# Q inside attention: four direct products, or seven products of sums

## The chip, the cores and the metric

The kernel runs on one core of a Trainium2 chip. The core has a matrix engine (TensorE: PE for its matmuls, PEld for its weight loads), VectorE (DVE), ScalarE (ACT), GpSimd (POOL) and a queue engine (SyncE, SP) that here issues nearly all DMAs. Matmuls read SBUF and write PSUM, of which the kernel uses eight banks of 128 x 512 floats. The metric is the time of one execution on the device in microseconds (us), lower is better. The kernel before takes 3028.04 us (median of 3 runs, 3027.93 to 3028.24).

## The reference

One transformer block over 2048 tokens of width 576, in float32. Six rows (shift, scale and gate, twice) come from `silu(c) @ w_mod`. Then

- `h = layernorm(x) * (1 + ca) + sa`
- `q = h @ wq`: 32 heads of 128; keys and values are the last 512 rows of a cache, 16 heads of each, so two query heads share a key and value head
- `p = softmax(q k^T / sqrt(128))`, `o = p v`, `x = x + ga * (o @ wo)`
- `h = layernorm(x) * (1 + cb) + sb`, and `x = x + gb * ((sigmoid(h @ w_gate) * (h @ w_up)) @ w_down)` with 4608 inner columns

## The kernel before

**Precision.** Float32 operands are split into a high part, rounded by ACT to the matmul's type, and the low rest (DVE or POOL subtracts). A product of two operands is three matmuls: high x low, low x high, high x high.

**Stages.** A short start, attention, output projection, and the gated MLP. Output projection and MLP already work with seven products where a 2 x 2 block product would take eight; the sums of their weights are made in the background, during attention. They are not changed.

**Attention.** Tokens come in four blocks of 512, in two halves of two blocks. The unit of order is a *block* `b`: one head over one block of tokens, 128 in all (`NBLK`), in the order of the list `seq`. A block has four *tiles* of 128 tokens, and the stage's loop runs over 512 tiles: `for n in range(NLO, N + TPB + 4)`, one *step* each, `N` = 512. `b, i = divmod(n, 4)`. In step `n` the program writes, in this order:

1. whatever is registered for the step with `at_n`
2. a quarter of Q of block `b + 2` (`qproj`): for a block 14 matmuls, four K-chunks of 128 rows at three each, and two for the remaining 64 rows. They accumulate in one bank (`qp`); after the last, ACT copies the high part, scaled by `QSCALE`, and DVE subtracts the low one (tile `qt`, two buffers)
3. the three score matmuls of tile `n + 2` and the row maximum on DVE (`neg<-st`)
4. four transposes of the exponentials of tile `n`, and their split (`ptt<-st`, ACT and then DVE)
5. the exponential of tile `n + 2` on ACT, with row sums; at a block's last tile DVE takes reciprocals (`rs<-sum`)
6. a quarter of PV of block `b - 1` (`pv`): three matmuls of 512 columns, over the tile `ptt` of that whole block, of which there are two. After the fourth quarter DVE multiplies the result by the reciprocals (`ov<-ot,rb`)
7. whatever is registered for the end of the step with `at_late`

Four banks (tag `st`) go round between scores and transposes, two (`ot`) between the PV of successive blocks, and one (`wo`) serves the background's small matmuls.

**The divisors.** The reciprocals lie along partitions, and PV's result needs them along columns. So SP stores them to DRAM (`put_rs`, tensor `rscr`) and loads them back spread over all partitions (`get_rs`, tile `rb`). SP works its queue in order; the load waits there until the store has landed.

**Q's weights.** For each head and each half, `load_q` fetches 576 x 128 weights, ACT makes the high part (`wa<-raw`) eight steps before their first use, and POOL the low part (two instructions) seven steps before.

**Background.** Between these, 79 weight jobs (36 `ab`, 9 `tail`, and 34 *wide* ones: 16 `wo`, 18 `down`) load weights into *rooms*, SBUF space of the four x blocks which is free during attention (tiles `x`), make sums and splits on POOL and ACT (`bg_sums`, `bg_split`), and store them to DRAM (`bg_store`). A loop (`free = {0: 9, ...`) writes out at which step each job starts, by when its room is free and by a due time (`due`) that paces them.

**What sets the order.** The tile framework draws the waits from what each instruction reads and writes, and places instructions on each engine as they become free by its own estimate; `keep_order` and `pin` fix an instruction behind all that the program wrote earlier for that engine. Every POOL instruction of the background is fixed so. The matmuls of Q, scores, transposes and PV are not. Nearly all instructions pass through one helper at line 36, so the profile shows L36 and they are told apart by their tiles.

## Time and profile before

| what | value |
|---|---|
| median of three runs | 3028.04 us |
| the profiled execution: its span, first to last instruction | 3026.5 us |
| the median less that span | 1.5 us |
| granted TensorE clock over the span | 0.999 |
| attention (start of the stage's loop to the output projection's first matmul, by TensorE's timeline) | ends at 1419.8 us |
| PE, DVE, ACT, POOL busy, of the span | 99%, 69%, 56%, 55% |
| Q matmuls in the groups | 1524 + 254, and 12 + 2 in the bank `wo` |

The profile's rows name an instruction by engine, operation, and out<-in by the program's tiles. `qp<-hTm,wa` are Q's matmuls (`hTt` for the 64 rows), `st<-kt,qt` scores, `st<-ident,pp` transposes, `ot<-ptt,vs` PV. A matmul's own duration includes its way through the array, which overlaps the next one's; the distance between starts is what it costs. "SPq" is SP's queue.

### The profile page before, as it was taken

How to read it: one execution, taken by the hardware profiler on the slowest of the kernel's cores; microseconds unless marked ns; L12 is line 12 of the kernel's file. 1: busy time of each engine (PE TensorE's matmuls, PEld its weight loads, DVE VectorE, ACT ScalarE, POOL GpSimd, SP SyncE). 2: the span in 40 equal slices, each digit the busy share in tenths (PEclk: the TensorE clock that was granted, in tenths of full speed). 3: DMA queues.
4: the chain of work that ended last, by engine and by line, in shares of the span. 5: the costliest groups of instructions: out<-in, count | busy, mean ns of one | idle time of the engine just before them, and what ended most of it. 6: DMA issues, size and time to landing. Idle time of an engine off the chain costs nothing.

```text
span 3026.5 us, 49171 instructions
## 1 busy us (share of the span) xinstructions
PE 3006.8 (99%) x16644; PEld 2592.7 (86%) x16644; DVE 2088.4 (69%) x3685; ACT 1695.8 (56%) x3424; POOL 1666.3 (55%) x1558
## 2 busy tenths in 40 slices
PE   8999999999999999999999999999999999999999
PEld 7888888888888888888999988888888888888888
DVE  6666666677666666667888867666666876666667
ACT  5666666657666676555444654444444544444443
POOL 2334457634577887412555127766655566655565
PEclk9999999999999999999999999999999999999999
DMA  4677777776777777775547656555555565555554
GB/s 127 189 197 217 196 224 227 227 210 183 207 233 236 240 248 247 211 215 177 193 159 306 224 189 192 155 155 166 168 148 144 161 204 140 143 148 142 144 138 119
DMA packets 485788, 571.32 MB, mean 189 GB/s; under 512 B 52000, under 2 KB 434208, under 8 KB 476832
## 3 DMA queue, kind: packets, MB, share of 16 engines
q1 hardware_dynamic: 484400, 567.65, 63.1%
q8 instruction: 132, 2.16, 0.3%
q14 instruction: 120, 0.98, 0.1%
q10 hardware_dynamic: 1136, 0.53, 0.1%
HBM read 394.33 MB, written 173.70 MB: 188 GB/s over the span
## 4 chain that ended last, share of the span: by engine, by line
PE 94%; DVE 2%; issue 1%; POOL 1%; DMA 1%; ACT 1%; SPq 0%; POOLq 0%; DVEq 0%; ACTq 0%
PE a L36 21%; PE st L36 18%; PE w L36 13%; PE qp L36 13%; PE ot L36 11%; PE c L36 11%; PE b L36 5%; DVE x L36 1%; POOL x L36 1%; PE wo L36 1%; SPq L36 0%; DVE ptt L36 0%; ACT pp L36 0%; DVE neg L36 0%; DVE hc L36 0%
## 5 line engine op out<-in xcount | busy, mean ns | idle before, releaser
L36 DVE TENSOR_TENSOR x<-w,x 128x288 f32<-128x288 f32 x964 | 421.4, 452 | 249.4 <-PE w L36 246.8
L36 PE MATMUL a<-hc,sw 128*128 128x512 f32 x2016 | 583.4, 395 | 1.4 <-DVE v L36 1.3
L36 DVE TENSOR_REDUCE neg<-st 128x1 f32<-128x512 f32 x512 | 352.4, 688 | 275.6 <-PE st L36 274.9
L36 ACT ACTIVATE ptt<-st 128x512 fp32r<-128x512 f32 x512 | 306.0, 598 | 391.0 <-PE st L36 390.0
L36 PE MATMUL ot<-ptt,vs 128*128 128x512 f32 x1536 | 483.5, 423 | 1.8 <-DVE ptt L36 1.7
L36 PE MATMUL st<-kt,qt 128*128 128x512 f32 x1536 | 443.4, 395 | 0.4 <-ACT pp L36 0.4
L36 PE MATMUL qp<-hTm,wa 128*128 128x512 f32 x1524 | 440.5, 398 | 2.3 <-DVE hTm L36 1.2
L36 DVE TENSOR_TENSOR ptt<-st,ptt 128x512 fp32r<-128x512 f32 x512 | 351.9, 688 | 126.6 <-ACT ptt L36 126.3
L36 PEld LDWEIGHTS a<-hc,sw 128*128 128x128 f32 x2016 | 356.4, 188 | 41.6 <-DVE v L36 2.8
L36 ACT ACTIVATE pp<-st,neg 128x512 f32<-128x512 f32 x512 | 350.4, 684 | 43.7 <-DVE neg L36 42.6
L36 ACT ACTIVATE sw<-sr 128x384 fp32r<-128x384 f32 x504 | 257.9, 519 | 189.1 <-issue 90.0
L36 POOL TENSOR_TENSOR sw<-sr,sw 128x256 fp32r<-128x256 f32 x245 | 200.4, 819 | 282.8 <-ACT sw L36 282.6
L36 PEld LDWEIGHTS st<-kt,qt 128*128 128x128 f32 x1536 | 286.7, 188 | 66.9 <-ACT pp L36 1.1
L36 PEld LDWEIGHTS w<-wh,hl 128*128 128x128 f32 x1776 | 297.2, 188 | 51.2 <-DVE x L36 2.7
L36 PEld LDWEIGHTS qp<-hTm,wa 128*128 128x128 f32 x1524 | 281.5, 188 | 69.5 <-DVE qt L36 7.1
L36 PE MATMUL w<-wh,hl 128*128 128x288 f32 x1776 | 327.5, 296 | 0.4 <-DVE x L36 0.3
L36 POOL TENSOR_TENSOR x<-x 128x256 f32<-128x256 f32 (+3 forms) x342 | 254.4, 763 | 117.8 <-DMA x<-in_B_w_up_dram 58.6
L36 PEld LDWEIGHTS st<-ident,pp 128*128 128x128 f32 x2048 | 254.3, 140 | 70.4 <-ACT pp L36 0.8
L36 PE MATMUL st<-ident,pp 128*128 128x128 f32 x2048 | 307.0, 273 | 0.5 <-DVE ptt L36 0.3
L36 PE MATMUL c<-hc,sw 128*128 128x512 f32 x1008 | 302.9, 394 | 0.0
L36 DVE TENSOR_TENSOR sw<-sr,sw 128x256 fp32r<-128x256 f32 x259 | 189.9, 733 | 141.0 <-ACT sw L36 113.2
L36 PEld LDWEIGHTS ot<-ptt,vs 128*128 128x128 f32 x1536 | 252.9, 190 | 30.7 <-DVE ptt L36 4.2
(239 smaller groups left out, 5043.6 us busy)
## 6 DMA issues: line engine op xcount, KB each, us to landing
sr<-wsc SPq DMA_DIRECT2D x504, 192.0 KB
wh<-dsc SPq DMA_DIRECT2D x144, 288.0 KB
dsc<-x SPq DMA_DIRECT2D x34, 1008.0 KB
vr<-oscr SPq DMA_DIRECT2D x32, 1024.0 KB
rb<-rscr SPq DMA_DIRECT2D x126, 256.0 KB
wsc<-x SPq DMA_DIRECT2D x36, 896.0 KB
oscr<-ov SPq DMA_DIRECT2D x63, 512.0 KB
wosc<-x SPq DMA_DIRECT2D x32, 1008.0 KB
```

The costliest lines, as they stand in the source:

```text
L36: i = got(*args, **kw)
```

## The change

In 30 *units* (all but the first eight blocks) Q is made for two heads and two blocks of tokens together. With the weights of the two heads as rows and the two halves of 512 K-rows as columns, the weights are A11, A12, A21, A22, the normalized tokens B11, B21, B12, B22, and the four results come from seven products of six matmuls instead of four times twelve; the 64 remaining rows add two matmuls to four of the products.

- The sums of the tokens (T1 to T4) are made once for each half, split, and stay in SBUF (the *planes*: the former `hTm` tiles, two further tiles for T1 and T2, and for T3 the fourth x block's space). The sums of the weights (S1 to S4) are made for each unit by POOL, each factor is split, high by ACT, low by POOL or (products 1 and 4) DVE.
- The products accumulate in the banks `qp` ("x") and `wo` ("y"); DVE adds them up over temporaries in SBUF and the last three blocks' Q is split from there. `QSCALE` moves into the keys.
- `QUOTA` says how many of a unit's 50 matmuls each of 14 steps gets; PV takes two steps of six matmuls instead of four of three, in those steps where Q has one or none.
- The exponentials lie in a ring of six tiles instead of two blocks of four, so one PV in three is cut into pieces.
- The divisors' store and load are written one step earlier each, since PV ends two steps earlier.
- Three rooms instead of four; the planner is written anew, jobs start at step 22 instead of 9, sums one step earlier after the load. The x rows for the second half go into rooms 0 and 1.
- The first two weight loads of the output projection go from 34 and 32 steps before the loop's end to 9 and 8, and the fourth x block's load to 9. One matmul is added ahead of the output projection.

The diff, cut to its core:

```diff
     def qproj(b, part):
...
-        lo, hi = n * part // 4, n * (part + 1) // 4
+        lo, hi = [n * i // 4 if b < 2 else (0, 0, 6, 13, 14)[i] for i in (part, part + 1)]
...
+    QSEQ = (("A11", "B11"), ("A12", "B21"), ("S2", "T2"), ("S3", "T3"), ("A22", "T4"), ("S1", "T1"), ("S4", "B22"))
+    QTAIL = {1: (0, 0), 4: (1, 0), 5: (1, 1), 6: (2, 1)}
...
+    def u_sum(u, to):
...
+        op = nc.gpsimd.tensor_add if to == "S1" else nc.gpsimd.tensor_sub
+        pin(op(UA[u, to], UA[u, x0], UA[u, x1]))
...
+    def u_hi(u, j):
+        t = USW[u, j] = wp.tile([P, 4, P], F32R, tag="sw", name="sw", bufs=4)
+        keep_order(nc.scalar.activation(t[:, 0:2], UA[u, QSEQ[j][0]], AF.Copy))
+
+    def u_lo(u, j):
+        t = USW[u, j]
+        eng = nc.vector if j in (1, 4) else nc.gpsimd
+        pin(eng.tensor_sub(t[:, 2:4], UA.pop((u, QSEQ[j][0])) if j > 5 else UA[u, QSEQ[j][0]], f32(t[:, 0:2])))
...
+    def u_out(b, eng):
+        t, c = q_tile(b), u_temp("c")
+        keep_order(nc.scalar.activation(t[:, 0, :], c, AF.Copy))
+        pin(eng.tensor_sub(t[:, 1, :], c, f32(t[:, 0, :])))
+
+    def u_end(u, j, n):
+        b = b_of(u)
+        x, y = UB.get((u, "x")), UB.get((u, "y"))
+        if j == 0:
+            keep_order(nc.scalar.activation(u_temp("m1"), y, AF.Copy))
+        elif j == 1:
+            t = q_tile(b)
+            keep_order(nc.scalar.activation(t[:, 0, :], y, AF.Copy))
+            nc.vector.tensor_sub(t[:, 1, :], y, f32(t[:, 0, :]))
+        elif j in (2, 3):
+            nc.vector.tensor_add(u_temp("u2" if j == 2 else "w"), x if j == 2 else y, u_temp("m1"))
+        else:
+            nc.vector.tensor_add(u_temp("c"), y if j == 4 else x, u_temp({4: "u2", 5: "w", 6: "m1"}[j]))
+            at_late(n + 3 if j == 6 else n, u_out, b + j - 3, nc.vector if j == 4 else nc.gpsimd)
+
+    def u_items(u):
+        for j, (a, c) in enumerate(QSEQ):
+            bank = "x" if j in (2, 5, 6) else "y"
...
+            fresh = j in (0, 2, 3)
...
+    QUOTA = (6, 6, 1, 0, 6, 6, 0, 0, 6, 6, 1, 0, 6, 6)
...
+    def u_some(n):
+        u, k = divmod(n - (TPB * b_of(0) - 10), 4 * TPB)
...
     def expo(n):
...
-                at_late(n - 1, put_rs, b)
-                at_late(n + 1, get_rs, b)
+                at_late(n - 2, put_rs, b)
+                at_late(n, get_rs, b)
...
     def transp(n):
...
+            PTT.append(at.tile([P, 6, 2, KT, P], F32R, tag="ptt", name="ptt", bufs=1))
...
+    def pv(b, part):
...
+        s0 = TPB * b % 6
+        pieces = [(0, s0, TPB)] if s0 + TPB <= 6 else [(0, s0, 6 - s0), (6 - s0, 0, s0 + TPB - 6)]
...
-    for hh in range(3, NH):
-        at_n(max(q_first(hh) - 12, -6), load_q, hh)
-        at_n(q_first(hh) - 8, split_q, hh)
-        at_n(q_first(hh) - 7, split_q_lo, hh)
...
+    for u in range(len(units)):
+        n = TPB * b_of(u) - 10
...
+        for i in range(4):
+            at_n(n - 5 + i, u_sum, u, f"S{i + 1}")
...
+        for j, m in enumerate((-4, -3, -1, 0, 3, 6, 8)):
+            at_n(n + m, u_hi, u, j)
+            at_n(n + m + 1, u_lo, u, j)
...
-    free = {0: 9, 1: 9, 2: 7, 3: 7}
-    n, due = 9, 9.0
...
+    LIFE = {"ab": (9, None), "tail": (13, None), "wo": (11, 6), "down": (11, 6), "mod": (12, None)}
...
+    n, due = 22, 22.0
...
-            at_n(n + 4 + part, bg_sums, k, part)
+            at_n(n + (4 if kind == "tail" else 3) + part, bg_sums, k, part)
...
-        due = max(due, n - 2) + {"ab": 4.6, "tail": 7.6}.get(kind, 5.9)
+        due = max(due, n - 2) + {"ab": 3.3, "tail": 5.4}.get(k[0], 4.3)
...
     for s in range(2):
-        at_n(N - 34 + 2 * s, w_load, 0, s)
+        at_n(N - 9 + s, w_load, 0, s)
...
+        u_some(n)
...
-        if ok(b - 1):
+        if ok(b - 1) and i < 2:
             pv(b - 1, i)
...
+    first = fpsum("b", 1, [P, BLK])
+    nc.tensor.matmul(first, VHL[0, 0][:, 0, 0, :], WHL[0, 0][0].rearrange("p a b -> p (a b)")[:, :BLK],
+                     start=True, stop=True)
```

More of the change, by code (lines that the diff above doesn't have):

```diff
@@ L97, in raw_tile @@
     def raw_tile(shape):
-        return wp.tile(shape, F32, tag="raw", name="raw", bufs=4)
+        return wp.tile(shape, F32, tag="raw", name="raw", bufs=2)
     def f32(ap):
@@ new lines, in adaln_block_kernel @@
+    QUOTA = (6, 6, 1, 0, 6, 6, 0, 0, 6, 6, 1, 0, 6, 6)
+    stream = {}
+    def u_some(n):
+        u, k = divmod(n - (TPB * b_of(0) - 10), 4 * TPB)
+        if not 0 <= u < len(units) or k >= len(QUOTA):
+            return
+        if k == 0:
+            stream[u] = u_items(u)
+        for _ in range(QUOTA[k]):
+            j = next(stream[u])
+            if j is not None:
+                u_end(u, j, n)
+        if k == len(QUOTA) - 1:
+            assert next(stream.pop(u), "end") == "end"
@@ new lines, in adaln_block_kernel @@
+    mod_at, mod_due = {}, [30, 52, 80, 116]
+    n, due = 22, 22.0
+    while jobs or wide or mods:
+        assert n < N - 30, (n, len(jobs), len(wide), len(mods))
+        if mods and n >= mod_due[4 - len(mods)]:
+            room = room_for(n, n + 12)
+            if room is not None:
+                key, m, add = mods.pop(0)
+                held_rooms[room].append((n, n + 12))
+                mod_at[key] = n
+                plan.append((n, ("mod", (key, m, add)), [room]))
+            n += room is None
+            continue
+        if due > n:
@@ L890, in adaln_block_kernel @@
             n += 1
             continue
-        k = (wide if two else jobs).pop(0)
+        k = None
+        if wide and n > mod_at.get("gate1" if wide[0][0] == "wo" else "gate", N) + 9 and \
+                len(wide) * 36 >= len(jobs) * 30:
+            k = wide[0]
+            r = room_for(n, n + LIFE["wo"][0])
+            h = room_for(n + LIFE["wo"][1], n + LIFE["wo"][0], r) if r is not None else None
+            rooms = None if h is None else [r, h]
+        if k is None or rooms is None:
+            k = jobs[0] if jobs else None
+            r = room_for(n, n + LIFE[k[0]][0]) if k else None
+            rooms = None if r is None else [r]
@@ L893, in adaln_block_kernel @@
+        if rooms is None:
+            n += 1
+            continue
+        (wide if len(rooms) == 2 else jobs).pop(0)
+        held_rooms[rooms[0]].append((n, n + LIFE[k[0]][0]))
+        if len(rooms) == 2:
+            held_rooms[rooms[1]].append((n + LIFE["wo"][1], n + LIFE["wo"][0]))
+        plan.append((n, k, rooms))
+        due = max(due, n - 2) + {"ab": 3.3, "tail": 5.4}.get(k[0], 4.3)
+    for n, k, rooms in plan:
         kind = k[0]
-        rooms = got[: 2 if two else 1]
-        for r in rooms:
-            free[r] = n + {"ab": 10, "tail": 14}.get(kind, 13)
+        if kind == "mod":
+            continue
```

333 lines of the change are left out of this document (237 added, 96 removed).

## The prediction

> **What bounds the kernel now.** I read the page's span and chain of waits first, then windows of the attention stage, then TensorE's timeline.
>
> ```profile
> span 3026.5 us, 49171 instructions
> PE 94%; DVE 2%; issue 1%; POOL 1%; DMA 1%; ACT 1%; SPq 0%; POOLq 0%; DVEq 0%; ACTq 0%
> 0.00:60.00 60.00, 51.62 (x254) 40.88 (x255) 39.10 (x98) 33.43 (x65) 18.05 (x27) 0.97 0.49 141
> 60.00:1437.00 1377.00, 1372.96 (x7100) 1127.69 (x7099) 944.90 (x1493) 894.52 (x1915) 739.28 (x719) 1.00 0.74 214
> 900.00:1100.00 200.00, 200.00 (x1030) 164.43 (x1030) 135.20 (x210) 138.35 (x286) 161.74 (x129) 1.00 0.77 237
> 1400.00:1440.00 40.00, 39.50 (x244) 34.25 (x243) 32.89 (x48) 20.51 (x42) 17.33 (x12) 1.00 0.75 285
> ```
>
> The window rows give the length, then the busy time of PE, PEld, DVE, ACT and POOL, the granted clock, the DMA share and GB/s. From 60 us to the end of attention PE is busy all but 4 us of 1377 at clock 1.00, so the stage lasts as long as its matmuls.
>
> A busy PE need not be at its pace, so I take the pace from starts. This is the timeline of TensorE over one block (four tiles) of attention, and two rows of the stage behind it:
>
> ```profile
> 939.78 0.84 PE L36 MATMUL st<-kt,qt 128*128 128x512 f32 x3
> 940.47 0.60 PE L36 MATMUL st<-ident,pp 128*128 128x128 f32 x4
> 940.82 0.95 PE L36 MATMUL ot<-ptt,vs 128*128 128x512 f32 x3
> 941.61 0.85 PE L36 MATMUL qp<-hTm,wa 128*128 128x512 f32 x3
> ...
> 944.12 1.09 PE L36 MATMUL qp<-hTm,wa 128*128 128x512 f32 x4
> 945.05 0.86 PE L36 MATMUL st<-kt,qt 128*128 128x512 f32 x3
> 945.76 0.60 PE L36 MATMUL st<-ident,pp 128*128 128x128 f32 x4
> ...
> 950.35 0.86 PE L36 MATMUL st<-kt,qt 128*128 128x512 f32 x3
> ...
> 1424.62 1.75 PE L36 MATMUL c<-wb,vh 128*128 128x288 f32 x12
> 1426.20 1.75 PE L36 MATMUL a<-wb,vh 128*128 128x288 f32 x12
> ```
>
> From 944.12 to 945.05 four 512-column matmuls start: 0.232 us each. Four transposes and three PV matmuls take 1.14 us (940.47 to 941.61), so four transposes take 0.44. A block has 12 score, 12 PV and 14 Q matmuls and 16 transposes: 38 x 0.232 + 4 x 0.44 = 10.58, and the trace has 950.35 - 939.78 = 10.57. Nothing is idle in it.
>
> **What the change takes from PE.** 30 units of four blocks each go from 4 x 14 = 56 Q matmuls to 7 x 6 + 4 x 2 = 50, all of 512 columns: 180 fewer, 180 x 0.232 = **41.8 us**. The first eight blocks keep theirs. A block becomes 10.57 - 1.5 x 0.232 = 10.22 us, a step 2.555.
>
> **What it adds to PE.** The ring of six tiles wraps inside block b when 4b mod 6 is 4, 43 blocks of 128; there 12 PV matmuls become 24 of 256 columns, for which no row stands. 288 columns take 1.58 / 12 = 0.132 (1424.62 to 1426.20), and with 0.232 at 512 the line through both gives 0.118 at 256: 24 x 0.118 - 12 x 0.232 = 0.05 a block, 2 us in all. Bounds: the transposes' 0.11 gives 43 x (2.64 - 2.784) = -6, the 288-column price 43 x (3.168 - 2.784) = +17. I take 2, since both neighbours lie on one line. The one matmul ahead of the output projection adds 0.2. The sum of PE's work is **-39.6**.
>
> **What it adds elsewhere.** Rows of the groups, with the mean ns of one ahead of the last bar:
>
> ```profile
> L36 DVE SCALAR_TENSOR_TENSOR qt<-qp,qt 128x512 fp32r<-128x512 f32 x127 | 87.5, 689 | 16.6 <-ACT qt L36 16.3
> L36 DVE TENSOR_TENSOR g<-c,g 128x512 f32<-128x512 f32 x72 | 49.0, 681 | 1.9 <-PE c L36 1.9
> L36 DVE TENSOR_TENSOR ov<-ot,rb 128x512 f32<-128x512 f32 x128 | 136.3, 1065 | 3.1 <-PE ot L36 3.1
> L36 POOL TENSOR_TENSOR sw<-sr,sw 128x256 fp32r<-128x256 f32 x245 | 200.4, 819 | 282.8 <-ACT sw L36 282.6
> L36 POOL TENSOR_TENSOR wa<-raw,wa 128x512 fp32r<-128x512 f32 x64 | 82.7, 1292 | 187.4 <-ACT wa L36 155.6 <-DMA wm<-in_w_mod_dram 18.5 <-issue 9.9
> L36 POOL TENSOR_TENSOR wa<-raw,wa 64x128 fp32r<-64x128 f32 x64 | 30.1, 470 | 5.0
> L36 POOL TENSOR_TENSOR x<-x 128x256 f32<-128x256 f32 x144 | 104.6, 746 | 53.7 <-DMA x<-in_B_w_up_dram 50.2
> L36 POOL TENSOR_TENSOR x<-x,gate 128x576 f32<-128x576 f32 x68 | 95.7, 1429 | 9.6 <-DMA x<-in_A_wo_dram 8.8
> ```
>
> DVE, per unit of 16 steps (40.9 us): four evacuations of 0.689 go; one of 0.69, five adds from PSUM of 0.68, one split and two weight splits of about 0.7 come: 6.2 - 2.8 = +3.4. DVE's 135.2 of 200 becomes 76%. ACT loses four copies of Q and two weight copies and gains five copies of Q and eight smaller ones, none over 0.7: at most +4 us per unit, 67% to 77%. Neither reaches PE.
>
> **POOL** loses per unit 2 x (1.29 + 0.47) = 3.5 and gains five weight splits of 0.82, four sums of 0.75, the tails' difference and split (0.47 and at most 1.3) and two splits of Q of 1.29: 11.4. Net +7.9, 237 over 30 units. The token planes add fourteen sums of 1024 columns (2 x 1.29 each) and four splits, 41 us. 739 + 237 + 41 = 1017 us. The planner now starts its weight jobs at step 22 and ends near 488, since three rooms hold fewer: 466 steps x 2.555 = 1191 us. POOL stands at 85% of that stretch if all fell inside it, against 62% (739 over the old 448 steps of 2.64). It runs strictly in written order. A wide job (output and down weights) holds it 2 x 1.43 + four sums + two splits, some 10 us over five steps, while a unit's weight split has two to four steps (5 to 10 us) before PE wants it; before, it had seven or eight. When a job meets a unit's splits, PE waits a microsecond or two. From 0 to 34 x 2 = 68; I take **5**, for the work of two steps that PE can run ahead of covers most such meetings.
>
> **The softmax divisors' trip** through DRAM: the reciprocals are stored, read back spread over partitions, and multiplied into PV's result. PV now ends two steps earlier after the reciprocals, and store and load each move one step up SP's queue.
>
> ```profile
> 944.92 0.18 DVE L36 RECIPROCAL rs<-sum 128x4 f32<-128x4 f32 x1
> 946.18 0.41 SPq L36 DMA_DIRECT2D rscr<-rs  x1
> 950.38 0.32 SPq L36 DMA_DIRECT2D rb<-rscr  x1
> 960.70 1.07 DVE L36 TENSOR_TENSOR ov<-ot,rb 128x512 f32<-128x512 f32 x1
> 691.44 3.15 DMA rb<-rscr
> SPq L36 <- DMA rscr<-rs: 229.3, 87, 6.0
> ```
>
> From reciprocal to multiplication there are 960.70 - 944.92 = 15.8 us, six steps; then four, 10.2. The trip needs 1.26 to the store, on average 229.3 / 87 = 2.6 and at most 6.0 for its landing, and 3.15 for the load (a row of the chain): 7.0 on average, 10.4 at worst. DVE, held by the multiplication, has the next reduction and split behind it, and PE the softmax two steps on. 0 to 126 x 0.2 = 25; I take **3**, for only the tail of the trips is late.
>
> The Trainium skill's DMA: Bandwidth & Descriptors, section "Anatomy of one DMA — SWDGE (gpsimd) path", gives every DMA a fixed 2 us or so, mostly the write's receipt, which a shorter step does not shorten; that speaks against the change. By it the estimated trip is 2 x 2.0 plus 0.6 for 256 KB, this term is 0, and the sum ends 3 us lower; the rows above are longer, and they decide.
>
> **Waits in the written order.** Two of a unit's products (the fifth and the seventh) add onto a bank right behind the matmul whose result DVE must read from it first. Behind the multiplication (1.065) and an add (0.68), less the matmul that runs meanwhile, that is 1.5 us at the one; at the other 1.065 + 0.68 less four matmuls, 0.8. And PV's first step asks for the block's last tile 0.44 + 0.70 + 0.44 = 1.58 us after its transposes began, where the split of their low part ends later:
>
> ```profile
> 947.02 0.69 DVE L36 TENSOR_TENSOR ptt<-st,ptt 128x512 fp32r<-128x512 f32 x1 [0.37 <-ACT ptt L36]
> ...
> 713.29 1.41 PE L36 MATMUL ot<-ptt,vs 128*128 128x512 f32 x5
> 714.54 0.92 PE L36 MATMUL qp<-hTm,wa 128*128 128x512 f32 x3
> ```
>
> 947.71 - 945.76 = 1.95, 0.37 short. As written, 30 x 2.3 + 120 x 0.37 = 113 us. But the emitted order isn't the written one: at 713.29 two PV matmuls of the next step ran ahead of three Q matmuls. The scores and transposes of the step and the next scores (0.70 + 0.44 + 0.70 = 1.84) are free to go ahead and cover 1.5. 0 to 113; I take **3**, as in the windows above, where such waits exist too and PE lost 4 us in 1377.
>
> **Start, middle, end.** The first 60 us hold 8.4 us of idle PE, so reordered early loads can gain or lose some 4. The loads ahead of the output projection move from 34 steps before its end to nine:
>
> ```profile
> vr<-oscr SPq DMA_DIRECT2D x32, 1024.0 KB
> wb<-wosc SPq DMA_DIRECT2D x12, 1152.0 KB
> x<-in_A_x_dram SPq DMA_DIRECT2D x5, 1152.0 KB
> ```
>
> One x block, five weight blocks and two of attention's outputs are 8960 KB, 9.2 MB: 32 us at the 285 GB/s of the window round the stage's end, 43 at attention's 214, against 13 steps or 33 us. Late by 0 to 10. Start and end together -4 to +14; I take **1**, the bursts at that place being the fast ones.
>
> Sum: -41.8 + 2 + 0.2 + 5 + 3 + 3 + 1 = -27.6. The profiled span of 3026.5 becomes 2998.9; the runs' median lies 1.5 over the span, so **3000.4 us**, -0.9%.
>
> **Rivals.**
> - *All waits hide*: 3028.0 - 39.6 = 2988. For it: PE's 1372.96 of 1377 now. Against: POOL's and SP's shorter leads.
> - *PE meets its waits as written*: a third of the 113 uncovered is 38, so 3026. For it: TensorE has less free work, since Q itself is what waits. Against: row 713.29.
> - *Every divisor trip is late*: 25 us, so 3013. For it: waits of 6.0; against: the mean of 2.6.
> - *256 columns cost what 288 do*: +15, so 3015. Against: the line through two widths.
> - *Slower, POOL sets the pace*: POOL's loads get three steps of lead, 7.7 us instead of 10.6. It already waited 53.7 us for one load's landing; if 3 us more are lost in each of 79 jobs, POOL needs 1017 + 54 + 237 = 1308 us where 1191 are there. Half of the excess met by PE, 58 us, gives 2988 + 58 = 3046. It decides from 40 us on.
>
> **Numbers.** Forecast 0.42 (its own range 2990 to 3012), all hidden 0.20, as written 0.09, trips 0.09, 256 columns 0.05, POOL 0.15. The range 2985 to 3026 holds all but POOL's and half of the as-written case; its low end is 2988 with some of the start's gain. About 0.2% (6 us) is what can be told from no change: below 3022 lie the forecast, the hidden, the trips and the columns cases and a part (0.04) of the as-written one, 0.80; 0.06 stays within; 0.14 is slower.
>
> **What the profile would show.** Right: Q matmuls down by 180, PE at 99% in every attention window, steps near 2.56 us, attention ending some 28 us earlier, the later stages unchanged. Wrong: idle PE ended by POOL's weight splits (POOL near 95% between 60 and 1300 us); DVE idle before the multiplication, ended by the divisors' load; idle before fifth and seventh products; 256-column starts over 0.12 us apart.

## The result, and the profile after

The changed kernel is slower: 3206.83 us (median of 4 runs, 3205.68 to 3211.55) against 3027.98 us (4 runs, 3027.76 to 3028.24). The ratio is 1.059, 95% interval 1.058 to 1.061. The forecast was 3000.4 us, its range ended at 3026.

From the page of the kernel after, the span and the shares of engines in the chain of waits that ended last:

```profile
span 3203.9 us, 50611 instructions
PE 49%; DVE 1%; POOL 1%; issue 0%; DMA 0%; ACT 0%; SPq 0%; DVEq 0%; POOLq 0%; ACTq 0%
```

Here the chain is followed back only to 1550 us, where attention is nearly over, so these shares (52% in all) say nothing of attention; the 94% of before reach back to the start and are not to be set against the 49%. First I ask whether TensorE got the work that was promised. These are TensorE's groups of the kernel after between 60 and 1600 us, shapes kept apart (busy time, mean ns of one, then the idle time before them and who ended it):

```profile
L36 PE MATMUL ot<-ptt,vs 128*128 128x512 f32 x1008 | 277.6, 411 | 5.6 <-DVE ptt L36 5.3
L36 PE MATMUL wo<-hTm,sw 128*128 128x512 f32 x540 | 164.2, 425 | 30.4 <-ACT m L36 15.5 <-POOL sw L36 8.2 <-DVE w L36 3.4
L36 PE MATMUL ot<-ptt,vs 128*128 128x256 f32 x1020 | 150.2, 294 | 8.1 <-DVE ptt L36 8.0
L36 PE MATMUL qp<-tpT,sw 128*128 128x512 f32 x360 | 118.3, 419 | 9.9 <-POOL sw L36 9.6 <-ACT sw L36 0.3
L36 PE MATMUL qp<-hTm,sw 128*128 128x512 f32 x180 | 57.2, 434 | 11.5 <-DVE c L36 11.1 <-POOL sw L36 0.3
L36 PE MATMUL wo<-tp,sw 128*128 128x512 f32 x180 | 55.2, 415 | 7.9 <-DVE qt L36 7.7
L36 PE MATMUL wo<-hTt,tw 128*128 128x512 f32 x120 | 46.4, 428 | 0.0
L36 PE MATMUL qp<-hTt,tw 128*128 128x512 f32 x120 | 38.4, 402 | 0.0
```

540 + 360 + 180 + 180 + 120 + 120 = 1500 matmuls for 30 units: 50 each, as written, 180 fewer than 30 x 56. The work did shrink. The windows of the same kernel say where the time went (length, then busy time of PE, PEld, DVE, ACT and POOL, granted clock, DMA share, GB/s):

```profile
60.00:1594.00 1534.00, 1399.16 (x7289) 1127.87 (x7288) 1033.02 (x1634) 939.61 (x2133) 972.94 (x986) 0.97 0.65 189
900.00:1100.00 200.00, 186.64 (x960) 149.82 (x959) 139.32 (x213) 128.33 (x287) 141.72 (x139) 0.97 0.69 205
1100.00:1300.00 200.00, 176.10 (x896) 140.75 (x894) 124.30 (x194) 112.96 (x256) 144.52 (x144) 0.95 0.68 204
```

Attention ends at 1594 us instead of 1420, and all but 3 us of the loss lies there (1609.8 us follow it in the span, 1606.7 before). TensorE is idle in each of these windows, and its clock is below 1.00 in each. No other engine is full: DVE is busy 1033 of 1534 us, 67%, and POOL, whose work grew most, 973 us, 63%.

To see what the time consists of I went through the starts of TensorE's matmuls from 60 us to PV's last one. Each distance to the next start is priced by its width: 232 ns for 512 columns, 127 for 256 (measured below), 110 for a transpose. What a distance has over its price is counted as half clock when it starts in a stretch in which the trace grants clock 0.50, else as a gap when it is over 0.15 us, else as rest.

| kernel | time, us | matmuls at price | gaps (number) | half clock | rest |
|---|---|---|---|---|---|
| before | 3028.0 | 1347.6 | 9.8 (29) | 0 | 2.1 |
| after | 3206.8 | 1314.8 | 170.3 (187) | 38.7 | 10.0 |

So 32.8 us were won at the matmuls and 207 us lost between them. 160 of these are gaps. The waits of the kernel after, 60 to 1600 us (who waits for whom: us in all, times, longest):

```profile
POOL qt L36 <- ACT qt L36: 126.9, 40, 12.9
ACT tw L36 <- POOL tr L36: 115.8, 28, 9.0
...
PE st L36 <- ACT pp L36: 51.3, 26, 7.0
...
PE wo L36 <- ACT m L36: 15.5, 15, 1.7
...
PE qp L36 <- POOL sw L36: 9.9, 5, 5.6
...
PE wo L36 <- POOL sw L36: 8.2, 8, 2.9
```

Two of these did not exist before: ACT stands 115.8 us for a sum that POOL makes (in attention of the kernel before, ACT waits for POOL 1.8 us in all), and POOL stands 126.9 us for ACT's copies of Q. TensorE's own largest wait is for the exponentials (`pp`), behind ACT; it also stands 18.1 us for POOL's weight splits (`sw`). One case of ACT's wait for the sum in the timeline, engine by engine (POOL, ACT, DVE, PE; in brackets the idle time before):

```profile
964.36 2.65 POOL L36 TENSOR_TENSOR x<-x,x 128x1152 fp32r<-128x1152 f32 x1
...
968.65 0.74 POOL L36 TENSOR_TENSOR sS<-q,sS 128x256 f32<-128x256 f32 x1
969.35 0.46 POOL L36 TENSOR_TENSOR tr<-tr 128x128 f32<-128x128 f32 x1
...
965.00 0.19 ACT L36 ACTIVATION_READ_ACCUMULATOR pp<-st,neg 128x1 f32 x1
969.84 0.52 ACT L36 ACTIVATE tw<-tr 128x384 fp32r<-128x384 f32 x1 [4.64 <-POOL tr L36]
970.27 0.91 ACT L36 ACTIVATE x<-x 128x864 fp32r<-128x864 f32 x1
971.08 0.58 ACT L36 ACTIVATE ptt<-st 128x512 fp32r<-128x512 f32 x1
...
971.69 0.69 DVE L36 TENSOR_TENSOR ptt<-st,ptt 128x512 fp32r<-128x512 f32 x1 [3.21 <-ACT ptt L36]
...
967.22 1.69 PE L36 MATMUL ot<-ptt,vs 128*128 128x256 f32 x12
968.74 1.32 PE L36 MATMUL wo<-hTm,sw 128*128 128x512 f32 x5
972.38 0.97 PE L36 MATMUL st<-kt,qt 128*128 128x512 f32 x3 [2.33 <-ACT pp L36]
974.63 2.63 PE L36 MATMUL wo<-hTm,sw 128*128 128x512 f32 x6 [0.85 <-ACT m L36]
977.06 1.48 PE L36 MATMUL st<-kt,qt 128*128 128x512 f32 x3
```

Read it from the top. POOL works off a background job in its written order; the small sum `tr` for the tails of Q's weights is behind it and comes at 969.35. ACT's copy of it (`tw`) is written in the same step and stands at the head of ACT's order, so ACT does nothing for 4.64 us. The copy of the transposes (`ptt`) and the exponentials are behind it; DVE waits 3.21 us for the one, TensorE 2.33 us for the other. Then six matmuls take 977.06 - 974.63 = 2.43 us, 0.405 each, where 0.232 is the pace. The windows round that place show the granted clock beside it:

```profile
972.00:975.00 3.00, 1.77 (x9) 1.31 (x10) 2.23 (x5) 3.00 (x9) 2.92 (x4) 1.00 1.05 425
975.00:978.00 3.00, 3.00 (x9) 2.32 (x8) 1.09 (x2) 1.37 (x4) 2.53 (x3) 0.50 0.96 353
```

After the gap the granted clock is 0.50. 20 such stretches lie in attention from 60 us on, none before. The same timeline gives the price of the 256-column pieces: twelve start between 967.22 and 968.74, 0.127 us each.

### The profile page after: what moved, and what is told of

Its sections match the earlier page's. It is cut to its first block, busy times and chain, and to the rows that moved or that the text cites. A ratio compares the mean times of both kernels' runs of the same rounds, so it can differ in the third digit from the quotient of the medians.

```text
span 3203.9 us, 50611 instructions
## 1 busy us (share of the span) xinstructions
PE 3052.6 (95%) x16981; PEld 2610.6 (81%) x16981; DVE 2190.0 (68%) x3845; ACT 1749.0 (55%) x3658; POOL 1914.0 (60%) x1836
## 4 chain that ended last, share of the span: by engine, by line
PE 49%; DVE 1%; POOL 1%; issue 0%; DMA 0%; ACT 0%; SPq 0%; DVEq 0%; POOLq 0%; ACTq 0%
PE a L36 20%; PE w L36 13%; PE c L36 10%; PE b L36 5%; PE ot L36 0%; DVE x L36 0%; PE st L36 0%; POOL x L36 0%; DVE v L36 0%; DMA rb<-rscr 0%; DVE sw L36 0%; POOL vs L36 0%; POOL hl L36 0%; DVE ov L36 0%; DVE ptt L36 0%
## 5 line engine op out<-in xcount | busy, mean ns | idle before, releaser
L36 PE MATMUL st<-kt,qt 128*128 128x512 f32 x1536 | 477.6, 414 | 52.8 <-ACT pp L36 50.0
L36 PE MATMUL ot<-ptt,vs 128*128 128x512 f32 (+1 forms) x2052 | 433.0, 352 | 13.7 <-DVE ptt L36 13.3
L36 PEld LDWEIGHTS a<-hc,sw 128*128 128x128 f32 x2016 | 355.9, 188 | 42.3 <-DVE v L36 3.3
L36 PEld LDWEIGHTS ot<-ptt,vs 128*128 128x128 f32 x2052 | 317.1, 192 | 61.4 <-DVE ptt L36 26.2
L36 POOL TENSOR_TENSOR x<-x 128x288 f32<-128x288 f32 (+5 forms) x369 | 287.7, 795 | 69.2 <-DMA x<-in_B_w_up_dram 41.0
L36 PEld LDWEIGHTS st<-ident,pp 128*128 128x128 f32 x2048 | 260.8, 142 | 79.7 <-issue 4.8
L36 PE MATMUL st<-ident,pp 128*128 128x128 f32 x2048 | 317.4, 276 | 3.2 <-DVE rs L36 2.1
L36 POOL TENSOR_TENSOR hl<-vs,hl 128x512 fp32r<-128x512 f32 x139 | 191.5, 1378 | 107.3 <-ACT hl L36 107.3
L36 POOL TENSOR_TENSOR x<-x,x 128x864 fp32r<-128x864 f32 (+3 forms) x111 | 207.4, 1874 | 68.6 <-ACT x L36 39.7
L36 PEld LDWEIGHTS c<-hc,sw 128*128 128x128 f32 x1008 | 181.5, 188 | 18.7
L36 PE MATMUL wo<-hTm,sw 128*128 128x512 f32 x540 | 164.2, 425 | 30.4 <-ACT m L36 15.5
```

The costliest lines, as they stand in the source:

```text
L36: i = got(*args, **kw)
```

## The experiments

All ran against the kernel before on the same chip (3026.3 to 3028.6 us). One row each, of the same kind as above; each was run once, and the four runs of the kernel after differ by 6 us among themselves, so a step of 5 or 6 us between two rows is not told from none. Where a kernel leaves work out, its section says so.

| kernel | time, us | matmuls at price | gaps (number) | half clock | rest |
|---|---|---|---|---|---|
| 1 tails earlier | 3157.9 | 1314.8 | 133.4 (165) | 32.6 | 6.2 |
| 2 no background sums on POOL | 3138.1 | 1316.9 | 112.4 (153) | 28.9 | 8.9 |
| 3 first + Q's last copies apart | 3151.9 | 1314.6 | 132.7 (163) | 26.4 | 6.8 |
| 4 third + order of products | 3139.0 | 1314.6 | 119.9 (124) | 27.6 | 5.6 |
| 5 before + PV in two steps | 3048.8 | 1356.3 | 24.6 (99) | 0 | -1.2 |
| 6 fourth + Q's low splits on DVE | 3112.6 | 1314.6 | 99.4 (124) | 23.2 | 5.0 |
| 7 sixth - background's computation | 3077.0 | 1314.8 | 78.9 (100) | 10.3 | 3.0 |
| 8 sixth + multiplication later | 3113.4 | 1315.1 | 100.7 (118) | 20.6 | 6.2 |
| 9 seventh + multiplication later | 3078.6 | 1315.1 | 70.8 (87) | 18.2 | 4.3 |
| 10 as 8, fixed in place | 3111.8 | 1315.1 | 91.6 (105) | 28.7 | 5.9 |
| 11 tenth + longer leads | 3120.0 | 1314.8 | 100.5 (105) | 27.9 | 5.4 |
| 12 seventh, five splits to POOL | 3071.9 | 1315.1 | 69.7 (87) | 14.4 | 2.9 |
| 13 fifth + load on DVE | 3053.5 | 1356.4 | 26.9 (77) | 0 | 6.6 |
| 14 twelfth + leads of 10 and 11 | 3062.2 | 1314.8 | 54.9 (77) | 13.4 | 6.0 |

**1. ACT held by the tails' sum.**

```diff
-        at_n(n - 9, u_load_tail, u)
+        at_n(n - 13, u_load_tail, u)
+        at_n(n - 7, u_sum_tail, u)
...
-        at_n(n - 2, u_sum_tail, u)
```

> The kernel after, with two lines moved: the tail weights of a unit are loaded 13 steps ahead instead of 9, and POOL makes their difference 7 steps ahead instead of 2; ACT's copy of it stays where it is. Theory A (ACT, working in written order, stands 115.8 us in 28 waits for POOL's difference, and the exponentials, the score banks and PE stand behind it): those waits fall under 15 us, PE's waits ended by ACT's exponential with them, most of the half-clock stretches go, and the time falls by 80 to 130 us, to 3075 to 3130. Theory B (POOL sets the pace, PE waits for its weight splits anyway): the time stays within 25 us of 3207. Theory C (the waits in the written order, banks and PV's last tile): within 25 us of 3207.

Measured: 3157.91 us, 48.9 less. ACT's wait for `tr` is no longer among its waits. Theory A had the wait right and its price too high (it asked for 80 to 130 us); B and C, within 25 us, fall as the whole account. One instruction of 0.46 us, written in the same step as the copy that needs it, cost more than the 27.6 us that the whole change was to win. But 130 us of the loss are still there.

**2. POOL's amount of work.** It starts from the kernel after and leaves out, during attention, the background's sums and gate products on POOL (all but those of six jobs) and its low splits, so the later stages multiply other weights.

```diff
     def bg_sums(k, part):
         kind, f = k
+        if kind != "ab" or f >= 6:
+            return
...
     def bg_split(k, part):
...
-        pin(nc.gpsimd.tensor_sub(v.bitcast(F32R), v, hi[:, a:b]))
```

> The kernel after, leaving out most of the background's work on POOL: the sums and gate products of all but the first six weight jobs, and all low splits of the weight jobs. Loads, ACT's high copies and stores stay, so the output is not the reference's. Theory A and theory B both say that POOL then keeps up: ACT's wait for the tail difference under 15 us, the divisors' and banks' waits stay, time 2990 to 3040. Theory C says that the time stays above 3120, since nothing of the Q order changed.

Measured: 3138.12 us, 68.7 less. From its windows, and its waits:

```profile
60.00:1530.00 1470.00, 1386.81 (x7325) 1124.27 (x7324) 1009.83 (x1637) 944.31 (x2139) 488.23 (x542) 0.98 0.66 198
...
POOL qt L36 <- ACT qt L36: 371.2, 54, 19.9
...
POOL sw L36 <- ACT sw L36: 274.4, 48, 13.3
...
ACT tw L36 <- POOL tr L36: 86.9, 28, 7.2
```

POOL is busy 488 of 1470 us, a third, and the kernel is still 110 us slower than before: its capacity does not set the pace. A and B, which both asked for 2990 to 3040, miss; the time lies where C put it, but the first experiment has shown that the waits of the banks are not the whole. Even with an idle POOL, ACT waits 86.9 us for `tr`, for POOL in turn stands in its written order behind splits that wait for ACT (371.2 and 274.4 us).

**3. Q's last copies taken apart.** The first experiment, the seventh product's sum in a temporary of its own, and POOL's low split of Q written two steps after ACT's copy instead of right behind it.

```diff
-            nc.vector.tensor_add(u_temp("c"), y if j == 4 else x, u_temp({4: "u2", 5: "w", 6: "m1"}[j]))
+            key = "w" if j == 6 else "c"
+            nc.vector.tensor_add(u_temp(key), y if j == 4 else x, u_temp({4: "u2", 5: "w", 6: "m1"}[j]))
...
+            at_n(n + 2, u_out_lo, b, eng, key)
```

> As e1_tail_early, and two more edits: the last Q sum of a unit goes into the temporary w instead of c, which POOL may still be reading, and POOL's low split of Q is written about a step and a half after ACT's copy instead of right behind it (POOL stood 126.9 us in 40 waits for that copy). Theory A: POOL's waits for ACT's copy of Q fall under 30 us, DVE's wait for POOL's read of c (22.8 us) goes, and the time is 20 to 50 us below e1_tail_early. Theory B: POOL's own work is unchanged, so within 10 us of e1_tail_early. Theory C: within 10 us of e1_tail_early.

Measured: 3151.89 us, 6 less than the first, where theory A asked for 20 to 50. The wait that it aimed at fell from 103.7 to 27.6 us and another has its place: TensorE's scores now wait for POOL's late split, 27.4 us in 12 gaps.

**4. The banks.** The third, with the products in another order, so that none adds onto a bank that DVE must read first (one unit, `old`, keeps the order).

```diff
+    def order(u):
+        return range(7) if old(u) else (0, 2, 1, 5, 3, 4, 6)
...
+            if j == 3 and not old(u):
+                nc.vector.tensor_add(u_temp("w"), x, u_temp("w"))
...
-        for j, m in enumerate((-4, -3, -1, 0, 3, 6, 8)):
+        for j, m in enumerate((-4, -3, -1, 0, 3, 6, 8) if old(u) else (-5, -2, -3, 3, 4, 1, 6)):
```

> The third experiment's kernel (tails' loads and sums earlier, the low split of Q by POOL two steps after ACT's copy), and the seven products of a unit in another order (first, third, second, sixth, fourth, fifth, seventh; quotas 6,6,1,1,6,6,1,1,6,8,0,0,4,4 instead of 6,6,1,0,6,6,0,0,6,6,1,0,6,6), so that no product adds onto a bank out of which DVE or ACT must have read in the same step. One unit, at the boundary of the halves, keeps the old order. Base 3151.9 us. Theory C (waits on the banks of the fifth and seventh product, as the prediction wrote them: 1.5 + 0.8 us a unit, 30 units): about 69 us go, 3083 +- 15, and the waits of Q's matmuls for DVE's c vanish. Rival D (two steps of six PV matmuls right behind the softmax of their block's last tile take from TensorE the work it could run ahead with, and the exponentials come late; the banks' waits only take the place of this one): no more than 20 us go, 3132 to 3155, and the excess ended by ACT's exponentials (pp) stays above 60 us in TensorE's starts.

Measured: 3139.03 us, 13 less; the waits for `c` at the banks are gone from TensorE's. That is a fifth of the 69 us that the prediction wrote out for them, and four times the 3 us that it took for all such waits; C, which asked for the 69, falls. The time is in D's range, but the exponentials end some 32 us of TensorE's gaps and not D's 60, so neither theory names the rest. What is on top now, in the waits and then in one case of the timeline (ACT, POOL, PE):

```profile
PEld st L36 <- POOL qt L36: 47.8, 18, 7.7
...
1158.96 0.62 ACT L36 ACTIVATE qt<-w 128x512 fp32r<-128x512 f32 x1
...
1164.48 1.47 POOL L36 TENSOR_TENSOR sx<-ov 128x512 f32<-128x512 f32 x1
...
1169.85 2.61 POOL L36 TENSOR_TENSOR x<-x,x 128x1152 fp32r<-128x1152 f32 x1
1172.41 1.26 POOL L36 TENSOR_TENSOR qt<-w,qt 128x512 fp32r<-128x512 f32 x1
...
1166.11 0.40 PE L36 MATMUL st<-kt,qt 128*128 128x512 f32 x1
1173.73 1.22 PE L36 MATMUL st<-kt,qt 128*128 128x512 f32 x2 [7.23 <-POOL qt L36]
```

Q's low split is 1.26 us of work, and ACT's copy of the same Q was done at 1159.6. But three sums over attention's outputs and a background split of 2.61 us are written ahead of it, and TensorE stands 7.23 us in the middle of a score.

**5. PV in two steps alone.** The kernel before with the ring of six tiles, PV in two steps, the divisors' DMAs a step earlier, and Q of a block in quotas that keep the steps equal. No products of sums, rooms and background as before.

```diff
-        lo, hi = n * part // 4, n * (part + 1) // 4
+        lo, hi = [n * i // 4 if b < 2 else (0, 0, 6, 13, 14)[i] for i in (part, part + 1)]
...
+            PTT.append(at.tile([P, 6, 2, KT, P], F32R, tag="ptt", name="ptt", bufs=1))
...
-        if ok(b - 1):
+        if ok(b - 1) and i < 2:
```

> The kernel before with one part of the change alone: the exponentials in the ring of six tiles, PV of a block in two steps of six matmuls (24 of 256 columns in one block of three), Q of a block in quotas of 0, 6, 7 and 1 matmuls by step so that steps stay equal, and the divisors' store and load one step earlier. No products of sums; weights of Q, rooms and background as before. Base 3028.0 us. Rival D (PV in two steps, with the order of steps that it brings, makes the loss): 3110 to 3160, idle TensorE in attention ended by the exponentials and by the transposes' split. Theory C (the loss belongs to Q's products: banks and the work they give ACT, DVE and POOL): at most 3043, that is 2 us for the pieces and up to 13 for late divisors and last tiles.

Measured: 3048.77 us, 20 more than before: 6 over C's bound and far from D, which falls. From its windows:

```profile
60.00:1440.00 1380.00, 1372.35 (x7469) 1138.47 (x7468) 923.29 (x1473) 856.65 (x1899) 732.58 (x714) 1.00 0.73 210
```

TensorE is busy 1372 of 1380 us at clock 1.00. The 256-column pieces are 1020 x 0.127 - 510 x 0.232 = 11.2 us of it, and small gaps 15 (the rest is 3 us lower, and 2 us of matmuls fell before 60 us). So this part of the change costs some, but neither the large gaps nor the half clock come from it alone: they come with the rest, the units and what was moved for them (three rooms, the new plan of the background).

**6. Q's low splits on DVE.** The fourth, with the last two of a unit's low splits of Q on DVE, right behind ACT's copy.

```diff
-                at_late(m, u_out, b + 2, nc.gpsimd, "w", m)
+                at_late(m, u_out, b + 2, nc.vector, "w", m)
...
-            at_late(m, u_out, b + j - 3, nc.vector if j == 4 else nc.gpsimd, key, m)
+            at_late(m, u_out, b + j - 3, nc.vector, key, m)
```

> The fourth experiment's kernel (tails early, other order of the products), and the low splits of Q of a unit's third and fourth block on VectorE right behind ACT's copy, as for the second block, instead of on POOL two steps later. Base 3139.0 us, in which TensorE's scores wait 42.7 us for POOL's low split of Q, the longest 7.2 us, behind POOL's background work. Theory P (POOL isn't too slow, but whatever stands in its written queue comes late behind a background job that itself waits for ACT): those 43 us go and some of the half clock behind them, 3080 to 3100. Rival V (VectorE, with 1.4 us more a unit, comes late to the transposes' split, and the wait only changes its name): 3125 to 3145, with waits for ptt by DVE above 40 us in TensorE's starts.

Measured: 3112.55 us, 26.5 less. The direction was theory P's, the size less than P asked. The 42.7 us of waits for POOL's split are gone, and TensorE's gaps ended by DVE's split of the transposes grew from 26 to 36 us: a part of what V expected.

**7. The background's computation.** The sixth, leaving out the background's sums and gate products (all but six jobs) and all its splits on ACT and POOL during attention; loads and stores stay, so the later stages multiply other weights.

```diff
     def bg_sums(k, part):
         kind, f = k
+        if kind != "ab" or f >= 6:
+            return
...
     def bg_split(k, part):
+        return
```

> The kernel of the sixth experiment, leaving out the background's computation during attention: the sums and gate products of all but the first six jobs on POOL, and all its splits on ACT and POOL; its loads and stores stay. The output is then another one. Theory B2 (what is left of the loss comes from the background meeting the units on ACT and POOL: waits of ACT for a store to leave a room, 33.2 us before, and late weight splits on POOL): 2990 to 3025, TensorE at 98% or more in every window of attention. Rival U (the units alone do it: their sums on VectorE and copies on ACT stand in the way of the softmax): within 30 us of the sixth experiment's time.

Measured: 3077.03 us, 35.5 less, between the two theories: of the 85 us that the sixth stood over the kernel before, two fifths came from the background's computation. The others stay without it, but not with the units alone: the background's loads and stores, its three rooms and the sums over the modulation's weights are still there. The longest single gap is of that kind, ACT and then TensorE:

```profile
386.03 0.53 ACT L36 ACTIVATE x<-x,cexp 128x288 f32<-128x288 f32 x1 [11.81 <-DMA x<-in_w_mod_dram]
...
389.44 0.48 PE L36 MATMUL st<-ident,raw 128*128 128x128 f32 x1 [10.06 <-ACT pp L36]
```

ACT waits 11.81 us for the load of a weight of the modulation, with the softmax behind it, and TensorE loses 10.06. No kernel here has the units without these loads and rooms, or the rooms and the new plan without the units, so what belongs to which stays open.

**8, 9, 10. The divisors.** In the sixth kernel DVE stands 38.3 us for the divisors' load. The eighth and ninth (the sixth and the seventh, the ninth thus with the background's computation left out) write the multiplication one step later; the tenth also fixes it there (`pin`; that line is the tenth's alone).

```diff
+                at_late(TPB * b + 6, scale_o, b)
...
-            nc.vector.tensor_mul(OT[unit][:, :, blk % 2, :],
+        pin(nc.vector.tensor_mul(OT[half, hd][:, :, blk % 2, :],
```

> The sixth experiment's kernel with the multiplication of PV's result by the divisors written one step (2.6 us) later. The bank of that result isn't needed again for five more steps. Base 3112.6 us, with 36.7 us of idle VectorE ahead of that multiplication, ended by the divisors' load. Theory T (the trip is late after the shorter PV, and VectorE, held in order, passes the delay to the softmax behind it): the 36.7 us fall below 8 and most of it comes off the time, 3078 to 3095. Rival N (VectorE's idle time there lies beside other waits and costs little): 3104 to 3118.

> The seventh experiment's kernel (the background's sums, gate products and splits left out, so another output), with the same multiplication one step later. Base 3077.0 us, with 36.2 us of idle VectorE before it. Theory T: 3042 to 3060. Rival N: 3069 to 3082. If T holds, the units with nothing behind them still stand 40 to 55 us over the 3003 us that 180 fewer matmuls and the pieces at 0.127 us give.

> The sixth experiment's kernel with the multiplication by the divisors one step later and fixed there behind what the program wrote for VectorE (in the eighth the framework was free to place it, and it stayed: 12.5 us behind the reciprocals, as without the edit). Base 3112.6 us, with 36.7 us of idle VectorE ended by the divisors' load. Theory T: the distance from reciprocals to multiplication grows by some 2.5 us, the idle time falls below 12, and 3078 to 3098 comes out. Rival N (that idle time lies beside other waits): 3104 to 3118 with the idle time gone.

DVE's wait for the load in the sixth, the eighth and the tenth:

```profile
DVE ov L36 <- DMA rb<-rscr: 38.3, 27, 3.5
...
DVE ov L36 <- DMA rb<-rscr: 54.2, 35, 3.8
...
DVE ov L36 <- DMA rb<-rscr: 11.3, 12, 2.9
```

Measured: 3113.41, 3078.59 and 3111.83 us. The eighth and ninth say nothing on the theory: unfixed, the multiplication stayed where it was (12.5 us behind the reciprocals in the median block, 12.4 in the sixth). The tenth does: 14.4 us behind them, the wait down by 27 us, and the time unchanged. Theory T falls: that idle time of DVE lay beside other waits.

**11. Longer leads at three places.** The tenth, with the sums of Q's weights three steps earlier, a wide job's second room a step later after its store, the modulation's sums two steps later after their load, and one of the weights' splits a step earlier.

```diff
-            at_n(n - 5 + i, u_sum, u, f"S{i + 1}")
+            at_n(n - 8 + i, u_sum, u, f"S{i + 1}")
...
-            at_n(n + 3 + c, lambda m, c: mod_sum(wm[m], c), m, c)
+            at_n(n + 5 + c, lambda m, c: mod_sum(wm[m], c), m, c)
```

> The tenth experiment's kernel with longer leads at the three other places where idle TensorE, followed back, began in the eighth: the sums of Q's weights three steps earlier on POOL (they stood behind the sums of attention's outputs and wide jobs, 9.4 us of TensorE in gaps over 0.8 us), a wide job's second room one step later after the store that leaves it (ACT held by that store, 10.1 us), and the sums over the modulation's weights two steps later after their load (ACT held by it, 8.8 us). Theory L (the units' order is sound, and the loss is a handful of instructions that wait at the head of an engine's written order with too short a lead): those 28 us go, and with the half clock behind them 30 to 50 below the tenth. Rival M (everything is too tight now, and a lead gained at one place is lost at the next): within 12 of the tenth.

Measured: 3119.99 us, 8 more than the tenth; rival M. Two of ACT's waits, first in the tenth, then in this one:

```profile
ACT x L36 <- DMA x<-in_w_mod_dram: 12.4, 7, 5.2
...
ACT x L36 <- DMA rscr<-rs: 8.4, 1, 8.4
```

```profile
ACT x L36 <- DMA rscr<-rs: 19.3, 3, 11.3
...
ACT x L36 <- DMA x<-in_w_mod_dram: 1.5, 1, 1.5
```

The wait for the modulation's load went, as meant, and one that the profile puts down to a store in SP's queue grew from 8.4 to 19.3 us.

**12, 13. DVE's load.** From the fifth to the sixth kernel DVE's work goes from 1.84 to 2.17 us a step. The twelfth (from the seventh, so the background's computation is left out) gives five of a unit's splits to POOL; the thirteenth (from the fifth, nothing left out) adds that much to a kernel without units, 240 reductions of 0.674 us.

```diff
-        eng = nc.vector if j in (1, 4) else nc.gpsimd
+        eng = nc.gpsimd
```

```diff
+        if 22 <= n < N - 10 and n % 2 == 0:
+            pin(nc.vector.tensor_reduce(idle, ident[:, None, :].to_broadcast([P, 4, P]), axis=AX.X, op=OP.max))
```

> The seventh experiment's kernel (without the background's sums, gate products and splits, so another output), with five of VectorE's splits a unit (two of the weights, three of Q) given to POOL, which is busy only 29% there. VectorE falls from 2.13 us a step by about 0.2. Base 3077.0 us. Theory V (VectorE's load: with the units it stands at 77% of a stretched step, would need 83% of a step of 2.555, and in written order each of its waits then comes out at TensorE): 3035 to 3057. Rival W (the units' order; VectorE's share is a consequence): 3070 to 3090, or worse by POOL's longer splits.

> The fifth experiment's kernel (PV in two steps alone, no products of sums) with one more reduction on VectorE every second step, over a constant, into a tile that nothing reads: 240 of about 0.65 us, 0.33 us a step, what the units add to VectorE between the fifth and the sixth experiment (1.83 to 2.17 us a step). The result is unchanged. Base 3048.8 us. Theory V: 3080 to 3115, with idle TensorE ended by ptt and pp. Rival W: at most 3058.

Windows of the seventh, the twelfth and the thirteenth:

```profile
60.00:1467.00 1407.00, 1347.10 (x7288) 1107.98 (x7288) 1051.04 (x1694) 877.51 (x2047) 414.64 (x480) 0.99 0.69 206
...
60.00:1462.00 1402.00, 1346.38 (x7289) 1109.33 (x7288) 972.62 (x1544) 875.94 (x2049) 562.20 (x630) 0.99 0.69 207
...
60.00:1450.00 1390.00, 1376.78 (x7468) 1138.26 (x7467) 1054.61 (x1713) 861.86 (x1899) 732.99 (x714) 1.00 0.71 209
```

Measured: 3071.90 us, 5 less, and 3053.45 us, 5 more, both where W put them and neither told from no change. In the thirteenth DVE is busy 1055 of 1390 us, 76%, as much as in the seventh (75%), and TensorE still runs at clock 1.00 with 1377 of 1390. Theory V falls from both sides: DVE's share of the time is not the cause. The added load waits for nobody and nobody for it, so this says nothing on DVE's work that does.

**14. The leads without the background.** The twelfth with the edits of the tenth and eleventh (the background's computation left out).

> The twelfth experiment's kernel (the background's sums, gate products and splits left out, so another output) with the edits of the tenth and eleventh: multiplication fixed one step later, sums of Q's weights three steps earlier, modulation's sums two steps later. Base 3071.9 us; TensorE's attention there is 1315 us of matmuls, 70 us in 87 gaps and 14 us of half clock; the three named origins make some 36 us of the gaps over 0.8 us. Theory L (a handful of heads of queues with short leads, and the background used up the slack in the eleventh): 3020 to 3045. Rival M (the gaps move on): 3062 to 3082.

Measured: 3062.19 us, 9.7 less. The gaps fall from 69.7 to 54.9 us, by 15, not by the 36 that the three origins held: the others moved on. It stands at M's edge.

No kernel with the units comes within 34 us of the kernel before.

## Why the prediction was wrong

By its own steps:

- **PE's work: right but for the pieces.** 180 fewer matmuls, 41.8 us, are in the groups. The pieces cost 11.2 us, not 2: 0.127 us each instead of 0.118, within the bounds of -6 and +17 and nearer to the rival at the 288-column price than to mine. The sign that I had named for it, starts over 0.12 us apart, is there. Together -30.6; the 32.8 of the table hold some 2 us of matmuls that fell before 60 us.
- **"Neither reaches PE" (ACT and DVE): the step that failed first.** I priced ACT's new copies by duration, at most 4 us a unit, and held that against its idle share. The price held: ACT is busy 940 us in the stage, and was 895 (up to 1437 us), 45 more where at most 120 were forecast. But I listed no wait of ACT. The tails' sum on POOL and ACT's copy of it are written in the same step, and I counted that sum under POOL's load only. Moved five steps ahead, with its load, it gave back 48.9 us (first experiment). DVE's load was mis-sized, 0.33 us a step between the fifth and the sixth kernel against 3.4 / 16 = 0.21, and its 76% should have read 78: (0.676 x 42.3 + 3.4) / 40.9. But load alone, even that much, costs no more than some 5 us (thirteenth).
- **POOL, 5 of 0 to 68: mis-sized, and for the wrong reason.** I looked at weight splits that PE wants and at capacity. The weight splits did hold TensorE, 18.1 us in the kernel after. But what moved the time was Q's low split behind background work, 6 + 26.5 us (third and sixth), and 35.5 us go when the background leaves ACT and POOL (seventh), a part of them ACT's. That this is 68 us, my worst case, is chance: that bound was made of other waits.
- **"POOL sets the pace", the rival on the slower side: the sign was right by luck, the mechanism wrong.** It said 3046. POOL is 63% busy, not near 95%, and with half of its work gone the kernel stays 110 us slower (second). Order, not amount, makes it late.
- **Waits in the written order, 3 of 0 to 113: the second step that failed.** The banks alone were 13 us. The reason that I gave for 3 was that in the windows of before PE lost 4 us in 1377. That row was measured with leads of seven and eight steps for weight splits, with Q as work that waits for nobody, and with the background in four rooms; the change took all three away. That it is these three is argued; no run gives one of them back alone. A row of before shows what an order hides, not what a different order will.
- **The divisors, 3 of 0 to 25: small, as far as shown.** DVE does stand for the load (29.9 us after), which I had named as a sign of being wrong, and taking 27 us of it away from the sixth kernel moved nothing (tenth). The sign was badly chosen: idle time off the path.
- **Not in the sum at all: the half clock**, 38.7 us. All terms were added as if a gap cost its own length only.
- **Start and end: in their range**, +3 us after attention.

What stays open: the fourteenth kernel, with units and hardly any background computation, still loses 54.9 us in 77 gaps and 13.4 to the clock, where before lost 9.8 and none. Followed back in the trace, the larger ones begin at different instructions (divisors, POOL's sums over the outputs, a load), and longer leads at the three largest origins recovered 15 of 36 us of gaps. That it is the tightness of the written order as a whole is argued from this, not shown; an order without these dependencies wasn't tried, nor the three rooms and the new plan without the units.

The steps add up, each against the one before: tails 48.9, Q's copies 6.0, banks 12.9, Q's splits 26.5, background 35.5, DVE's splits 5.1, leads 9.7: 144.6 us, from 3206.8 to 3062.2, part of it half clock behind the gaps that went. Only the first four keep all the work: 94.3 us of the 178.9 that the change lost come back by the order and the choice of engine alone, and the last 50.3 with the background's computation left out. Each step was measured only behind the ones before it, and those of 5 and 6 us are not told from none.

## What to carry to other kernels

In a kernel whose engines run in written order, price each added instruction twice: by its duration, and by what stands behind it if its input is late. List the new producer-to-consumer pairs across engines and the number of steps between them, smallest first; the pair with none cost more than the whole gain here, at engines 61 to 67% busy. An engine that is 99% busy shows that its present order hides its waits; here it paid for some new gaps twice, in the gap and in the clock behind it.

## What the runs showed of the hardware

- **Gaps of about 2 us can be followed by half the clock.** In attention of the kernel after, each of the 14 gaps of TensorE over 2.6 us, and 7 of the 18 between 1.5 and 2.6, have a stretch of 3.4 or 6.8 us at clock 0.50 that begins in them or within 5 us behind them; 92 us in all, 38.7 us lost. The other 11 have none, so length alone does not decide it. Nor is 2.6 us an edge: in the other kernels some gaps of 2.6 to 3.3 us have none either. The case of 2.33 us is shown above. The Trainium skill's "TensorE: Matmul & The Clock Gate" ("Why this matters for your kernels") asks for no gaps over some 3 us; here some gaps of two thirds of that, and less, were followed by the half clock too.
- **DVE's splits stretch beside POOL.** A split of 256 columns with both inputs in SBUF takes 0.41 us on the mean where POOL is idle (16 of them in the kernel after) and 0.99 us where POOL works throughout (39); of 512 columns (Q's splits) 0.68 and 1.19. In the groups of the kernel after and of the seventh, where POOL does little:

```profile
L36 DVE TENSOR_TENSOR sw<-q,sw 128x256 fp32r<-128x256 f32 x60 | 47.9, 798 | 0.0
...
L36 DVE TENSOR_TENSOR sw<-q,sw 128x256 fp32r<-128x256 f32 x60 | 29.1, 485 | 0.0
```

  The Trainium skill's "SBUF — State Buffer" ("Who interferes with whom") has a port pair that such an operation of DVE and GpSimd lock against each other; the traces agree. I had priced these splits at about 0.7 us, from rows whose inputs came from PSUM.
